# Linear attention, cosine FFN and soft MoE in one kernel: when the w_out tiles of the first blocks are converted, and how they meet phi

## The chip, the core and the metric

The kernel runs on one core of a Trainium2 chip. Five engines work from queues of their own: TensorE (PE, with its weight loads shown as PEld), VectorE (DVE), ScalarE (ACT), GpSimd (POOL) and SyncE (SP, which here only issues DMAs). The metric is the device time of one execution in microseconds, the median of three runs for the kernel before.

## What is computed

```python
# q, k, v: (8, 8, 576, 64); everything is fp32
kv = einsum('bhsd,bhse->bhde', k, v)
out = einsum('bhsd,bhde->bhse', q, kv)
x = out / sqrt(mean(out * out, -1) + 1e-6) * g_norm        # -> (4608, 512)
h = x @ w_in                                               # (4608, 2048)
x2 = (h * cos(h)) @ w_out                                  # (4608, 512)
logits = x2 @ phi                                          # (4608, 32)
d = softmax(logits, axis=0)                                # over the tokens
c = softmax(logits, axis=1)                                # over the slots
slots = (d.T @ x2).reshape(8, 4, 512)
slot_out[e] = relu(slots[e] @ w1[e]) @ w2[e]
return c @ slot_out.reshape(32, 512)
```

`w_in` and `w_out` come in as float64 values whose bits the kernel turns into fp32 itself.

## The kernel before

The 4608 tokens are twelve blocks j of 384 tokens. A block's x is held transposed as a high and a low part (`xt`), and the 2048 columns of `w_in` are sixteen tiles f of 128. One main step (j, f) is `main`: 12 products of 128 x 128 weights with 384 tokens (high x high, high x low, low x high, four chunks each) into one PSUM bank `h`. Then ScalarE scales and rounds (`fr_tt`), VectorE takes the remainder (`round_off`, L403), ScalarE the sine (`cos_b`), VectorE multiplies by h (`cos_c`, L417) into `gT`.

`w_out` is never multiplied out for each token: the logits are gT times the small matrix wp = w_out @ phi, one 128 x 32 piece per tile f. `wp_kk` (L320) and `wp_sum` (L329) make that piece: four products with 32 columns of phi as weights, each into its own group of 32 PSUM partitions, a copy to SBUF (`wq`), and a product with `rep32`, which adds the four groups; a copy stores the piece in `wp`. `logits2` (L468) multiplies two tiles' gT with their pieces, block 0 into partitions 0 to 63 and block 1 into 64 to 127 of one bank (`l`).

Blocks 0 and 1 are interleaved: step f of the start does main step (0, f) and, from f = 4 on (`L=4`), (1, f-4). In the same steps the sixteen tiles of `w_in` (letters A R P L H S: scale on ScalarE, three bit operations on VectorE, high part on ScalarE, low part on GpSimd) and of `w_out` (a r p l: scale on ScalarE, the three bit operations on VectorE) are converted. The order inside a step is written out by hand in the strings `one` (steps 0 to 3) and `two`, and before step 0 in `start`; each letter is one call. `LI` and `LO` say how many tiles ahead of the step w_in and w_out are converted. Side work is hung on steps by `at2`: `wp_kk(f)` on step f + `wT` = f, `wp_sum(f)` on f + `wM` = f + 1, `logits2(j, f)` on f + 3 + 4j, the transposition of gT (`gtr`) one or two steps after its main step. The raw w_out tiles wait in three buffers (`ro`), so a load on SP's queue waits until the tile three before it is converted, and what is behind it on that queue waits too.

In the start the first batch's kv products, `att_out` (`ops`), `att_xs`, `att_xT` (`xTps`) and `att_lo` prepare block 0's x. The second batch's kv products run in step 0; `ke` says which engine copies them from PSUM (0 ScalarE, 1 VectorE).

Of the kernel before, what the change touches and what calls it, by code (L numbers as in the profile page):

```python
# [19 lines left out]
SIGN_BIT = -0x80000000  # L20

PLAN = dict(
    ke=(0, 1),
    lp=(0, 0, 0),
    wE=0,
    gE=(0, 0),
    nt=(1, (12, 16, 20, 24), (1, 2), (2, 1), (3, 1), 4),
    rx=0,
    nq=(0, 0),
    nl=3,  # L30
    wT=0,
    wM=1,
    E=((20, 21, 5, 1), (17, 19, 4, 2)),
    F=((23, 25), (22, 24)),
    L=4,
    LI=2,
    LO=2,
    PI=2,
    PO=2,
    PS=1,  # L40
    stop=None,
    start=(
# [17 lines left out]
    A=(((1, 2, 2), (1, 1, 1), (3, 3, 4), (0, 1, 0)), ((9, 10, 12), (0, 0, 0), (11, 13, 14), (0, 0, 0)), ((8, 11, 11), (1, 1, 1), (11, 14, 14), (1, 0, 0))),  # L60
# [14 lines left out]
def tile_linear_attention__ffn_cos__soft_moe(  # L75
# [15 lines left out]
    nc = tc.nc  # L91
    B, H, D = kv.shape[0], 8, 64
    NF, KD = w_in.shape[0], w_in.shape[2]
    NS = phi.shape[2]
    NB = qT.shape[0]
    TB = qT.shape[3]

    SP = 2
    const = ctx.enter_context(tc.tile_pool(name="const", bufs=1))
# [36 lines left out]
    def at_bank(name):  # L136
        return ps_a.tile([128, 512], F32, tag="at", name=name)

    def copy_on(e, out, in_):
        (nc.vector.tensor_copy if e else nc.scalar.copy)(out=out, in_=in_)  # L140
# [9 lines left out]
        return [(0, 64, 2 * p), (64, 64, 2 * p + 1)]  # L150

    def load_q(j):
        t = q_p.tile([128, 4, TB], F32, tag=f"q{j % 2}", name="q")
        if j == 0:
            for t3 in range(3):
                nc.sync.dma_start(out=t[:, :, t3 * 128:(t3 + 1) * 128], in_=qT[j][:, :, t3 * 128:(t3 + 1) * 128])
        else:
            nc.sync.dma_start(out=t, in_=qT[j])
        q_t[j] = t
# [38 lines left out]
    def att_out(j, t):  # L198
        ps = at_bank("ops")
        for pr in range(4):  # L200
            for p0, n, b in spans(j):
                assert (b, pr) in kv_done
                c0 = t * 128 + p0
                nc.tensor.matmul(out=ps[p0:p0 + n, pr * 128:(pr + 1) * 128],  # L204
                                 lhsT=q_t[j][:, pr, c0:c0 + n], rhs=kvbd[b % 2][:, pr, :],
                                 start=True, stop=True)
# [55 lines left out]
    first = {}  # L262

    def stage():
        ta = t_p.tile([128, 6, 512], F32, tag="TA", name="st_a")
        tb = t_p.tile([128, 6, 512], F32, tag="TB", name="st_b")
        sp = const.tile([128, SP, 512], F32, tag="sp", name="st_m")
        first["sx"] = x_p.tile([128, 6, 512], F32, tag="x1", name="st_x")
        first["sp"] = sp
        first["ex"] = const.tile([128, 512], F32, tag="ex", name="st_n")  # L270
        first["wi"] = [sp[:, i, :] for i in range(2)]
        first["wo"] = [ta[:, i, :] for i in range(3)]
        tf = ta.rearrange("p a c -> p (a c)")
        first["wq"] = [tf[:, 1536 + 128 * i:1664 + 128 * i] for i in range(2)]
        ring.extend([None, tf[:, 1792 + TB * i:1792 + TB * (i + 1)], 1] for i in range(3))
        first["ro"] = [tb[:, 2 * i:2 * i + 2, :].rearrange("p a c -> p (a c)").bitcast(I32).rearrange(
            "p (c t) -> p c t", t=2) for i in range(3)]

    def load_wout(f):
        t = first["ro"][f % 3]  # L280
        nc.sync.dma_start(out=t, in_=w_outT[f].bitcast(I32).rearrange("p k (c t) -> p (k c) t", t=2))
        raw_t[NF + f] = t
        loaded.add(NF + f)
# [31 lines left out]
        hi, lo = (w_t[f][:, i].rearrange("p k c -> p (k c)") for i in range(2))  # L315
        nc.gpsimd.tensor_tensor(out=lo, in0=T, in1=hi.bitcast(F32), op=ALU.subtract)  # L316

    wq_t, wp_done = {}, set()

    def wp_kk(f):  # L320
        assert ("L", f, 1) in done
        ps = at_bank("wps")
        for kk in range(KD):
            nc.tensor.matmul(out=ps[32 * kk:32 * kk + 32, 0:128], lhsT=phi_sb[:, kk, :],
                             rhs=first["wo"][f % 3][:, kk * 128:(kk + 1) * 128], start=True, stop=True)
        copy_on(PLAN["wE"], first["wq"][f % 2], ps[:, 0:128])
        wq_t[f] = ps

    def wp_sum(f):  # L329
        ps = wq_t.pop(f)[:, 128:128 + NS]  # L330
        nc.tensor.matmul(out=ps, lhsT=first["wq"][f % 2], rhs=rep32, start=True, stop=True)
        nc.scalar.copy(out=wp[:, f, :], in_=ps)
        wp_done.add(f)

# [456 lines left out]
    def at2(j, f, *a):  # L791
        at(*U(j, f), *a)
# [14 lines left out]
    def ld_at(j, f, fn, *a):  # L807
        loads.setdefault(U(j, f), []).append((fn, a))

    for j in range(NB):  # L810
        for f in range(NF):
            if on_pe(j, f):
                at2(j, f + (1 if j == 1 and f < NF // 2 else 2), gtr, j, f)
        for h in range(2):
            if (j, h) == (NB - 2, 1):
                for x in range(4):
                    ld_at(NB - 1, x + PLAN["lag"], regroup, j, h, (x,))
            elif not on_pe(j, 8 * h):
                for x in range(4):
                    ld_at(j, PLAN["rg"][h] + x * PLAN["rx"], regroup, j, h, (x,))  # L820
        if j == 0:
            for f in range(NF):
                at2(0, f + PLAN["wT"], wp_kk, f)
                at2(0, f + PLAN["wM"], wp_sum, f)
        if j < 2:
            for f in range(0, NF, 2):
                late_in = j and f + 3 + L >= NF - (L < 6)
                at2(*((1, f + 3) if late_in else (0, f + 3 + L * j)), logits2, j, f)
        if j < NB - 1:
            for c in range(4 * (j > 1)):  # L830
# [150 lines left out]
    with tc.manual_schedule():  # L981
        stage()
        make_identity(nc, ident)
        nc.vector.memset(mhalf, -0.5)
        for i in range(2):
            nc.vector.memset(kz[64 - 64 * i:128 - 64 * i, i], 0.0)
        for t in kvab:
            nc.gpsimd.memset(t, 0.0)
        for t in PLAN["start"].split():
            token(t, 0)  # L990
            if t == "q.0":
                nc.sync.dma_start(out=gn, in_=gn2)
                nc.sync.dma_start(out=phi_sb, in_=phi)
        nc.vector.tensor_reduce(out=rep32, in_=ident.rearrange("p (j s) -> p s j", s=NS), axis=AX.X, op=ALU.add)
        nc.vector.tensor_copy(out=rep, in_=rep32.rearrange("p (o s) -> p o s", o=1).to_broadcast([128, 4, NS]))
        for f in range(NF):
            if f + PLAN["LI"] + 2 < NF and f + PLAN["LI"] + 2 not in loaded:
                ld_at(0, f, load_win, f + PLAN["LI"] + 2)
            if f + PLAN["LO"] + 1 < NF and f + PLAN["LO"] + 1 + NF not in loaded:
                ld_at(0, f, load_wout, f + PLAN["LO"] + 1)  # L1000
        for f in range(NF):
            for t in (PLAN["one"] if f < L else PLAN["two"]).split():
                token(t, f)
# [25 lines left out]
def _lay_out(q, k, v, g_norm, moe_w_in, moe_w_out, moe2_phi, moe2_w1, moe2_w2):  # L1029
# [6 lines left out]
    for p in range(B // 2):  # L1036
# [8 lines left out]
    w_out = moe_w_out.reshape(16, P, 512)  # L1045
    w_outT = moe_w_out.reshape(16, P, 4, P).transpose(0, 3, 2, 1)
    return {
        "qT": np.stack(blocks),
        "kv": kvm,
        "kvr": kvr,  # L1050
        "gn2": np.concatenate([g_norm, g_norm]).reshape(P, 1),
# [31 lines left out]
```

## Time and profile before

| | us |
|---|---|
| median of three runs | 705.47 (705.43 to 707.11) |
| the profiled execution, its own time | 705.78 |
| its span, first to last instruction | 703.9 |

The rows below come from that one execution. In the rows of a time line the columns are the start, how long it took, engine, line, operation, output<-input, shape, count and, in brackets, the engine's idle time before and what ended it. TensorE's products in fp32 take two passes each, those of `h` (fp32r) and transpositions one. A table by stage shows for each stretch its length, then busy time and instructions of each engine, the granted TensorE clock as a share of the upper of its two levels (2.4 GHz; the lower is 1.2), the DMA share and GB/s. In the chain of waits each piece is start, length, engine, tile and line.

### The profile page before, as it was taken

To read this page: it belongs to the slowest core of one execution; us is meant where nothing else is said; L and a number is where in the kernel's file an instruction comes from. 1 tells how busy PE (TensorE), PEld (TensorE's weight loads), DVE (VectorE), ACT (ScalarE), POOL (GpSimd) and SP (SyncE) were. 2 spreads that over 40 slices of the span, in tenths; PEclk is the share of its full clock that TensorE was granted. 3 is DMA by queue.
4 is the path that set the end of the run, shared out by engine and by line. 5 is a ranking of instruction groups with operands and counts; after the bars stand their busy time and mean duration, and the time that the engine had idled before them with its cause. 6 is when DMAs were issued, how large, how long until landed. Compare 5 with 4: busy or idle time off the path is not lost.

```text
span 703.9 us, 13646 instructions
## 1 busy us (share of the span) xinstructions
PE 675.8 (96%) x5103; PEld 558.7 (79%) x5103; DVE 525.1 (75%) x1100; ACT 441.6 (63%) x931; POOL 106.2 (15%) x104
## 2 busy tenths in 40 slices
PE   7769999999999999999999999999999999999994
PEld 6659998886988887988888879888978787874364
DVE  3998998467888878888888888888887875444144
ACT  3577998675667675675576765756757567661143
POOL 2342333100402111112012021110120210000500
PEclk9999999999999999999999999999999999999996
DMA  9963442022742674574435845735349278989998
GB/s 316 393 209 132 180 171 100 1 85 96 209 130 76 186 187 140 168 198 107 136 81 159 208 141 160 213 93 150 85 108 327 70 233 268 346 302 346 393 360 358
DMA packets 69297, 134.12 MB, mean 191 GB/s; under 512 B 8433, under 2 KB 41841, under 8 KB 68465
## 3 DMA queue, kind: packets, MB, share of 16 engines
q1 hardware_dynamic: 69232, 133.27, 59.7%
q8 instruction: 40, 0.66, 0.4%
q14 instruction: 25, 0.20, 0.1%
HBM read 91.29 MB, written 13.63 MB: 149 GB/s over the span
## 4 chain that ended last, share of the span: by engine, by line
PE 71%; DVE 12%; ACT 10%; DMA 4%; issue 2%; SPq 0%; DVEq 0%; ACTq 0%
PE h L378 43%; PE ab L553 5%; PE l L465 4%; PE ops L204 3%; DVE gT L417 3%; ACT fr L408 3%; DVE tt L403 2%; PE xTps L236 2%; DVE tr L423 2%; PE tr L438 2%; PE eo L706 2%; PE eh L680 2%; ACT L408 1%; ACT L513 1%; DMA st_b<-in_w_outT 1%
## 5 line engine op out<-in xcount | busy, mean ns | idle before, releaser
L378 PE MATMUL h<-xt,w 128*128 128x384 f32 x2304 | 438.7, 342 | 1.0 <-DVE xt L249 0.4
L378 PEld LDWEIGHTS h<-xt,w 128*128 128x128 f32 x2304 | 397.0, 188 | 31.6 <-issue 12.2
L408 ACT ACTIVATE fr<-tt 128x384 f32<-128x384 f32 x192 | 100.4, 524 | 135.8 <-DVE tt L403 135.4
L417 DVE TENSOR_TENSOR gT<-fr,h 128x384 f32<-128x384 f32 x186 | 102.7, 553 | 58.3 <-ACT fr L408 58.1
L216 POOL TENSOR_TENSOR ri<-ss,mhalf 128x8 f32<-128x8 f32 x36 | 65.6, 1826 | 421.4 <-DVE ss L214 421.4
L403 DVE SCALAR_TENSOR_TENSOR tt<-tt,fr 128x384 f32<-128x384 f32 x192 | 106.1, 557 | 25.9 <-ACT tt L398 24.4
L398 ACT ACTIVATE tt<-fr 128x384 f32<-128x384 f32 x192 | 100.8, 525 | 6.1
L396 ACT ACTIVATE fr<-h 128x384 f32<-128x384 f32 x192 | 92.3, 481 | 14.2 <-PE h L378 14.1
L423 DVE STREAM_TRANSPOSE tr<-gT 128x384 f32<-128x384 f32 x144 | 83.3, 579 | 5.1 <-DVE gT L417 0.2
L240 ACT ACTIVATE xt<-xTps,gn 128x512 fp32r<-128x512 f32 x36 | 24.5, 683 | 25.8 <-PE xTps L236 25.8
L204 PE MATMUL ops<-kvA,q 128*64 128x128 f32 (+1 forms) x384 | 38.2, 278 | 1.4 <-ACT g L140 1.3
L204 PEld LDWEIGHTS ops<-kvA,q 128*64 128x64 f32 (+1 forms) x384 | 33.8, 164 | 5.4 <-issue 2.8
L249 DVE SCALAR_TENSOR_TENSOR xt<-xTps,gn,xt 128x512 fp32r<-128x512 f32 x36 | 26.4, 738 | 12.0 <-ACT xt L240 11.8
L316 POOL TENSOR_TENSOR w<-st_m,w 128x512 fp32r<-128x512 f32 x16 | 26.4, 1648 | 53.8 <-ACT w L311 42.1
L553 PE MATMUL ab<-g,d 128*32 128x512 f32 x288 | 33.5, 596 | 0.4 <-DVE d L535 0.4
L465 PE MATMUL l<-gT,wp 128*32 128x384 f32 x312 | 33.3, 498 | 0.0
L140 ACT COPY g<-tr 128x384 f32<-128x384 f32 (+1 forms) x64 | 23.4, 392 | 6.7 <-PE tr L438 6.3
L184 PEld LDWEIGHTS kvps<-kv 128*64 128x64 f32 x512 | 17.6, 138 | 11.8 <-issue 7.0
L213 DVE TENSOR_REDUCE ss<-sq 128x8 f32<-128x512 f32 x33 | 22.1, 671 | 5.0 <-ACT sq L211 4.8
L184 PE MATMUL kvps<-kv 128*64 128x64 f32 x512 | 20.7, 226 | 3.7 <-DMA kv<-in_kv 2.0
L225 DVE TENSOR_TENSOR xs<-ops,ri 128x512 f32<-128x512 f32 x33 | 22.3, 681 | 2.4 <-POOL ri L216 2.4
L211 ACT ACTIVATE sq<-ops 128x512 f32<-128x512 f32 x33 | 19.5, 590 | 7.2 <-PE ops L204 7.2
(139 smaller groups left out, 626.3 us busy)
## 6 DMA issues: line engine op xcount, KB each, us to landing
g<-tr SPq DMA_DIRECT2D x288, 96.0 KB
kv<-in_kv SPq DMA_DIRECT2D x32, 512.0 KB
ew<-in_w SPq DMA_DIRECT2D x19, 512.0 KB
out<-ot SPq DMA_DIRECT2D x12, 768.0 KB
q<-in_qT SPq DMA_DIRECT2D x11, 768.0 KB
rw<-in_w_in SPq DMA_DIRECT2D x16, 512.0 KB
st_b<-in_w_outT SPq DMA_DIRECT2D x16, 512.0 KB
ew<-in_w SPq DMA_DIRECT2D x6, 1024.0 KB
```

Of the source, the lines that this page charges most:

```text
L184: nc.tensor.matmul(out=ps[h], lhsT=t[:, 0, r, h], rhs=t[:, 1, r, h], start=(r == 0), stop=False)
L204: nc.tensor.matmul(out=ps[p0:p0 + n, pr * 128:(pr + 1) * 128], lhsT=q_t[j][:, pr, c0:c0 + n], rhs=kvbd[b % 2][:, pr, :], start=True, stop= ...
L216: nc.gpsimd.tensor_tensor(out=ri[:, :, 0], in0=ss, in1=mhalf, op=ALU.pow)
L378: nc.tensor.matmul(out=ps, lhsT=w[:, a, kk, :], rhs=x[:, b, kk, :], start=(n == 0), stop=(n == 3 * KD - 1))
L396: nc.scalar.activation(out=fr, in_=ps, func=AF.Copy, bias=0.25, scale=INV_2PI)
L398: nc.scalar.activation(out=tt, in_=fr, func=AF.Copy, bias=ROUND_M)
L403: nc.vector.scalar_tensor_tensor(out=tt, in0=tt, scalar=-ROUND_M, in1=fr, op0=ALU.add, op1=ALU.subtract)
L408: nc.scalar.activation(out=fr, in_=tt, func=AF.Sin, scale=-TWO_PI_DOWN)
L417: nc.vector.tensor_tensor(out=g, in0=fr, in1=h_t.pop((j, f)), op=ALU.mult)
L423: nc.vector.transpose(out=tr_t[j, h][:, :, o, :], in_=g.rearrange("p (b t) -> p b t", t=32))
L465: nc.tensor.matmul(out=l_t[j][32 * o:32 * o + 32, :], lhsT=wp[:, f, :], rhs=gT_t.pop((j, f)), start=(c == 0), stop=(c == (2 if j == NB - 1 ...
L553: nc.tensor.matmul(out=ps[32 * c:32 * c + 32, :], lhsT=d[:, t, :], rhs=gs[c // 2][t][:, (c % 2) * 512:(c % 2) * 512 + 512], start=(t == 0) ...
```

## The change

w_out tile f is converted in step f instead of f - 2 (`LO=0`, `PO=0`), so the calls a.0 to l.1 leave `start`, and the last two tiles are converted in steps 14 and 15. Its product with phi stands in step f + 2 (`wT=2`) and is made in another way: the four chunks of the tile are the weights (128 x 128 each), phi's 32 columns move, and the four products add up in PSUM; `wp_sum`, the copy `wq` and its product with `rep32` are gone. The logits of block 0 stand one step later (f + 4); those of block 1 stay (f + 7). The copies of the second batch's kv go to ScalarE. q is laid out by 128 tokens, so that the first block's three loads have segments of 2 KB instead of 512 B. A sine on a small constant stands first in ScalarE's queue, `rep32` and `rep` are made at the start, the last raw tile has a buffer of its own, gT has one more buffer (the space of `wq`), and one transposition (block 1, f = 8) stands a step later.

```diff
 PLAN:
-    ke=(0, 1),
+    ke=(0, 0),
-    wE=0,
-    wT=0,
-    wM=1,
+    wT=2,
-    LO=2,
+    LO=0,
-    PO=2,
+    PO=0,
 start:
-        "lo.0 xs.2 A.1 H.0 S.0 warm.4 a.0 lo.1 xT.2 warm.8 R.1 P.1 r.0 win.3 a.1 L.1 lo.2 H.1 r.1 p.0 S.1 p.1 "
-        "l.0 l.1 "
+        "lo.0 xs.2 A.1 H.0 S.0 warm.4 lo.1 xT.2 warm.8 R.1 P.1 win.3 L.1 lo.2 H.1 S.1 "
...
-        t = q_p.tile([128, 4, TB], F32, tag=f"q{j % 2}", name="q")
+        t = q_p.tile([128, 3, 4, 128], F32, tag=f"q{j % 2}", name="q")
-                nc.sync.dma_start(out=t[:, :, t3 * 128:(t3 + 1) * 128], in_=qT[j][:, :, t3 * 128:(t3 + 1) * 128])
+                nc.sync.dma_start(out=t[:, t3], in_=qT[j][:, t3])
...
     def wp_kk(f):
         assert ("L", f, 1) in done
-        ps = at_bank("wps")
+        ps = at_bank("wps")[:, 0:NS]
         for kk in range(KD):
-            nc.tensor.matmul(out=ps[32 * kk:32 * kk + 32, 0:128], lhsT=phi_sb[:, kk, :],
-                             rhs=first["wo"][f % 3][:, kk * 128:(kk + 1) * 128], start=True, stop=True)
-        copy_on(PLAN["wE"], first["wq"][f % 2], ps[:, 0:128])
-        wq_t[f] = ps
-
-    def wp_sum(f):
-        ps = wq_t.pop(f)[:, 128:128 + NS]
-        nc.tensor.matmul(out=ps, lhsT=first["wq"][f % 2], rhs=rep32, start=True, stop=True)
+            nc.tensor.matmul(out=ps, lhsT=first["wo"][f % 3][:, kk * 128:(kk + 1) * 128], rhs=phi_sb[:, kk, :],
+                             start=(kk == 0), stop=(kk == KD - 1))
         nc.scalar.copy(out=wp[:, f, :], in_=ps)
...
-                at2(j, f + (1 if j == 1 and f < NF // 2 else 2), gtr, j, f)
+                at2(j, f + (1 if j == 1 and f < NF // 2 else 3 if (j, f) == (1, NF // 2) else 2), gtr, j, f)
...
-                at2(*((1, f + 3) if late_in else (0, f + 3 + L * j)), logits2, j, f)
+                at2(*((1, f + 3) if late_in else (0, f + 4 + (L - 1) * j)), logits2, j, f)
...
+        table = sm_p.tile([128, 2], F32, tag="sb", name="table")
+        nc.scalar.activation(out=table[:, 0:1], in_=mhalf[:, 0:1], func=AF.Sin)
```

TensorE's queue of the kernel before, from the main products of step 5 of the interleaved blocks to those of step 7 (`tr` transposes gT, `wps` is the product with phi, `l` the logits, `h` the main products):

```order
L378 MATMUL h<-xt,w 128x384 x24
L438 MATMUL tr<-ident,gT 128x128 x6
L331 MATMUL wps<-rep_106,st_a 128x32
L324 MATMUL wps<-st_a,phi_sb 32x128 x4
L378 MATMUL h<-xt,w 128x384 x24
L438 MATMUL tr<-ident,st_a 128x128 x3
L438 MATMUL tr<-ident,gT 128x128 x3
L331 MATMUL wps<-rep_106,st_a 128x32
L324 MATMUL wps<-st_a,phi_sb 32x128 x4
L474 MATMUL l<-gT,wp 32x384 x3
L474 MATMUL l<-st_a,wp 32x384
L378 MATMUL h<-xt,w 128x384 x24
```

The same place in the changed kernel:

```order
L369 MATMUL h<-xt,w 128x384 x24
L429 MATMUL tr<-ident,gT 128x128 x6
L321 MATMUL wps<-phi_sb,st_a 128x32 x4
L465 MATMUL l<-gT,wp 32x384 x2
L369 MATMUL h<-xt,w 128x384 x24
L429 MATMUL tr<-ident,st_a 128x128 x3
L429 MATMUL tr<-ident,gT 128x128 x3
L321 MATMUL wps<-phi_sb,st_a 128x32 x4
L465 MATMUL l<-gT,wp 32x384
L465 MATMUL l<-st_a,wp 32x384
L369 MATMUL h<-xt,w 128x384 x24
```

The products with phi of one tile stand as four 128-wide ones in a row, and the two blocks' logits, which stood as four products in every other step, stand as two in every step.

VectorE's queue of the kernel before, from the second w_in tile's bit operations to gT of step 0 (`st_m` is a w_in tile, `st_a` a w_out tile, `xt` the low part of x, `kvA` the second batch's kv, `tt` and `gT` step 0's):

```order
L305 SCALAR_TENSOR_TENSOR st_m<-rw,st_m 128x512
L249 SCALAR_TENSOR_TENSOR xt<-xTps,gn,xt 128x4x128
L295 TENSOR_SCALAR st_a<-st_a 128x512
L300 SCALAR_TENSOR_TENSOR st_a<-st_b,st_a 128x512 x2
L305 SCALAR_TENSOR_TENSOR st_a<-st_b,st_a 128x512 x2
L994 TENSOR_REDUCE rep_106<-ident 128x32
L995 COPY rep<-rep_106 128x128
L295 TENSOR_SCALAR st_m<-st_m 128x512
L300 SCALAR_TENSOR_TENSOR st_m<-rw,st_m 128x512
L403 SCALAR_TENSOR_TENSOR tt<-tt,fr 128x384
L305 SCALAR_TENSOR_TENSOR st_m<-rw,st_m 128x512
L295 TENSOR_SCALAR st_a<-st_a 128x512
```

The same place in the changed kernel:

```order
L302 SCALAR_TENSOR_TENSOR st_m<-rw,st_m 128x512
L245 SCALAR_TENSOR_TENSOR xt<-xTps,gn,xt 128x4x128
L292 TENSOR_SCALAR st_m<-st_m 128x512
L297 SCALAR_TENSOR_TENSOR st_m<-rw,st_m 128x512
L394 SCALAR_TENSOR_TENSOR tt<-tt,fr 128x384
L302 SCALAR_TENSOR_TENSOR st_m<-rw,st_m 128x512
L292 TENSOR_SCALAR st_a<-st_a 128x512
L297 SCALAR_TENSOR_TENSOR st_a<-st_b,st_a 128x512
L408 TENSOR_TENSOR gT<-fr,h 128x384
```

The bit operations of two w_out tiles and the two `rep` instructions no longer stand ahead of the third w_in tile, and no copies of kvA stand ahead of gT.

## Rows read from the trace of the kernel before

**Rows 1.** The page: busy time of TensorE, share of the span, instructions.

```profile
PE 675.8 (96%) x5103; PEld 558.7 (79%) x5103; DVE 525.1 (75%) x1100; ACT 441.6 (63%) x931; POOL 106.2 (15%) x104
```

**Rows 2.** The table by stage: PE, PEld, DVE, ACT, POOL, clock, DMA.

```profile
24.00:47.50 23.50, 17.40 (x200) 15.63 (x199) 23.05 (x48) 16.66 (x36) 8.90 (x6) 1.00 0.76 283
47.50:53.30 5.80, 2.70 (x25) 1.61 (x21) 5.77 (x10) 2.80 (x7) 2.34 (x3) 1.00 0.84 256
53.30:60.20 6.90, 6.88 (x39) 6.79 (x38) 5.32 (x9) 3.56 (x8) 1.18 (x1) 0.75 0.45 164
...
71.90:113.00 41.10, 41.10 (x316) 37.32 (x317) 40.62 (x71) 38.71 (x105) 12.81 (x7) 1.00 0.46 165
113.00:130.00 17.00, 17.00 (x132) 14.70 (x129) 11.60 (x23) 11.38 (x27) 5.11 (x3) 1.00 0.19 64
...
147.00:640.00 493.00, 490.05 (x3542) 411.09 (x3544) 381.53 (x847) 317.81 (x645) 52.98 (x36) 1.00 0.58 169
```

**Rows 3.** The chain that ended last, in order of time: start, length, what.

```profile
54.37 5.40 PE h L378 x24
...
60.60 0.63 PE l L474 x4
...
66.74 4.39 PE h L378 x24
...
71.78 0.14 PE wps L331 x2
71.93 0.36 PE wps L324 x8
72.28 0.65 PE l L474 x8
...
126.48 0.77 PE l L474 x4
```

**Rows 4.** The time line of TensorE's products: one step, and the tail.

```profile
59.93 0.31 PE L331 MATMUL wps<-rep,st_a 128*128 128x32 f32 x2
...
642.24 0.98 PE L668 MATMUL sT<-rep,part 128*128 128x32 f32 x8
643.05 0.69 PE L643 MATMUL warm<-ident 128*128 128x128 f32 x4
```

**Rows 5.** The source line L331: passes, with shortest, median and longest in ns.

```profile
L331 PE MATMUL wps<-rep,st_a x32: 192/235/277, 34.6 to 130.1; 128*128 128x32 f32 x32
```

**Rows 6.** The time line of GpSimd and VectorE, 20 to 36 us.

```profile
20.90 1.33 POOL L316 TENSOR_TENSOR w<-st_m,w 128x512 fp32r<-128x512 f32 x1 [1.75 <-ACT w L311]
21.13 1.65 DVE L300 SCALAR_TENSOR_TENSOR st_m<-rw,st_m 128x512 int32<-128x512 int32 x1
...
28.69 0.42 DVE L295 TENSOR_SCALAR st_m<-st_m 128x512 int32<-128x512 int32 x1
29.15 0.69 DVE L300 SCALAR_TENSOR_TENSOR st_m<-rw,st_m 128x512 int32<-128x512 int32 x1
29.76 0.55 DVE L403 SCALAR_TENSOR_TENSOR tt<-tt,fr 128x384 f32<-128x384 f32 x1
...
31.16 1.92 DVE L140 COPY kvA<-kvps 64x64 f32<-64x64 f32 x8
...
33.83 0.55 DVE L417 TENSOR_TENSOR gT<-fr,h 128x384 f32<-128x384 f32 x1
...
35.97 0.55 DVE L403 SCALAR_TENSOR_TENSOR tt<-tt,fr 128x384 f32<-128x384 f32 x1
```

**Rows 7.** The time line of ScalarE, 23 to 27 us.

```profile
23.05 0.69 ACT L290 ACTIVATE st_a<-st_b 128x512 f32<-128x512 f32 x1 [0.98 <-DMA st_b<-in_w_outT]
...
24.34 0.66 ACT L290 ACTIVATE st_m<-rw 128x512 f32<-128x512 f32 x1
...
26.65 0.49 ACT L396 ACTIVATE fr<-h 128x384 f32<-128x384 f32 x1 [1.64 <-PE h L378]
```

More of the change, by code (lines that the diff above doesn't have):

```diff
@@ L95, in tile_linear_attention__ffn_cos__soft_moe @@
     NB = qT.shape[0]
-    TB = qT.shape[3]
+    TB = qT.shape[2] * qT.shape[4]
     SP = 2
@@ L202, in att_out @@
                 assert (b, pr) in kv_done
-                c0 = t * 128 + p0
                 nc.tensor.matmul(out=ps[p0:p0 + n, pr * 128:(pr + 1) * 128],
-                                 lhsT=q_t[j][:, pr, c0:c0 + n], rhs=kvbd[b % 2][:, pr, :],
+                                 lhsT=q_t[j][:, t, pr, p0:p0 + n], rhs=kvbd[b % 2][:, pr, :],
                                  start=True, stop=True)
@@ L273, in stage @@
         tf = ta.rearrange("p a c -> p (a c)")
-        first["wq"] = [tf[:, 1536 + 128 * i:1664 + 128 * i] for i in range(2)]
-        ring.extend([None, tf[:, 1792 + TB * i:1792 + TB * (i + 1)], 1] for i in range(3))
+        ring.extend([None, tf[:, 1536 + TB * i:1536 + TB * (i + 1)], 1] for i in range(4))
         first["ro"] = [tb[:, 2 * i:2 * i + 2, :].rearrange("p a c -> p (a c)").bitcast(I32).rearrange(
@@ L280, in load_wout @@
         t = first["ro"][f % 3]
+        if f == NF - 1:
+            t = q_p.tile([128, KD * 128, 2], I32, tag="q1", name="st_q")
         nc.sync.dma_start(out=t, in_=w_outT[f].bitcast(I32).rearrange("p k (c t) -> p (k c) t", t=2))
@@ L316, in cv_lo @@
         nc.gpsimd.tensor_tensor(out=lo, in0=T, in1=hi.bitcast(F32), op=ALU.subtract)
-    wq_t, wp_done = {}, set()
+    wp_done = set()
     def wp_kk(f):
         assert ("L", f, 1) in done
-        ps = at_bank("wps")
+        ps = at_bank("wps")[:, 0:NS]
         for kk in range(KD):
-            nc.tensor.matmul(out=ps[32 * kk:32 * kk + 32, 0:128], lhsT=phi_sb[:, kk, :],
-                             rhs=first["wo"][f % 3][:, kk * 128:(kk + 1) * 128], start=True, stop=True)
-        copy_on(PLAN["wE"], first["wq"][f % 2], ps[:, 0:128])
-        wq_t[f] = ps
-    def wp_sum(f):
-        ps = wq_t.pop(f)[:, 128:128 + NS]
-        nc.tensor.matmul(out=ps, lhsT=first["wq"][f % 2], rhs=rep32, start=True, stop=True)
+            nc.tensor.matmul(out=ps, lhsT=first["wo"][f % 3][:, kk * 128:(kk + 1) * 128], rhs=phi_sb[:, kk, :],
+                             start=(kk == 0), stop=(kk == KD - 1))
         nc.scalar.copy(out=wp[:, f, :], in_=ps)
@@ L823, in tile_linear_attention__ffn_cos__soft_moe @@
                 at2(0, f + PLAN["wT"], wp_kk, f)
-                at2(0, f + PLAN["wM"], wp_sum, f)
         if j < 2:
@@ L984, in tile_linear_attention__ffn_cos__soft_moe @@
         nc.vector.memset(mhalf, -0.5)
+        table = sm_p.tile([128, 2], F32, tag="sb", name="table")
+        nc.scalar.activation(out=table[:, 0:1], in_=mhalf[:, 0:1], func=AF.Sin)
+        nc.vector.tensor_reduce(out=rep32, in_=ident.rearrange("p (j s) -> p s j", s=NS), axis=AX.X, op=ALU.add)
+        nc.vector.tensor_copy(out=rep, in_=rep32.rearrange("p (o s) -> p o s", o=1).to_broadcast([128, 4, NS]))
         for i in range(2):
@@ L993, in tile_linear_attention__ffn_cos__soft_moe @@
                 nc.sync.dma_start(out=phi_sb, in_=phi)
-        nc.vector.tensor_reduce(out=rep32, in_=ident.rearrange("p (j s) -> p s j", s=NS), axis=AX.X, op=ALU.add)
-        nc.vector.tensor_copy(out=rep, in_=rep32.rearrange("p (o s) -> p o s", o=1).to_broadcast([128, 4, NS]))
         for f in range(NF):
@@ L998, in tile_linear_attention__ffn_cos__soft_moe @@
                 ld_at(0, f, load_win, f + PLAN["LI"] + 2)
-            if f + PLAN["LO"] + 1 < NF and f + PLAN["LO"] + 1 + NF not in loaded:
-                ld_at(0, f, load_wout, f + PLAN["LO"] + 1)
+            if f + PLAN["LO"] + 2 < NF and f + PLAN["LO"] + 2 + NF not in loaded:
+                ld_at(0, f, load_wout, f + PLAN["LO"] + 2)
         for f in range(NF):
@@ L1047, in _lay_out @@
     return {
-        "qT": np.stack(blocks),
+        "qT": np.stack(blocks).reshape(12, P, 4, 3, P).transpose(0, 1, 3, 2, 4),
         "kv": kvm,
```

## The prediction

> **What bounds the kernel now.** I read the page first: TensorE is busy 96% of the span [rows 1]. Then the stage table, since the diff touches only the start and the two interleaved blocks. In it the stretch from 24 to 53.3 us belongs to VectorE, busy 23.05 of 23.50 and 5.77 of 5.80 us, while TensorE has 2.70 of 5.80 in its second part. From there the roles change: TensorE is busy 41.10 of 41.10 us between 71.9 and 113, and 17.00 of 17.00 up to 130 [rows 2]. VectorE is nearly full there too (40.62), but TensorE shows no wait, and the pieces of the chain of waits are TensorE's alone, step after step: transpositions, `wps`, sometimes `l`, then 24 passes of `h` in 4.39 us [rows 3]. After the interleaved blocks TensorE stays busy 490.05 of 493.00 us [rows 2], so a shift at 147 us is handed to the end undiminished. Hence two rules for the sum: until about 54 us, count what delays VectorE; from 54 us to the last main step of the second block, count TensorE time.
>
> **The start (gain).** Six VectorE instructions of the tiles 0 and 1 of `w_out` and the eight copies of the second batch (1.92 us) leave VectorE's queue, with `rep` put ahead of all data, where VectorE is still idle. The gain isn't their sum, because VectorE then waits for others. Step by step, from [rows 6, 7]: the L300 that ends at 22.78 is followed at once by L305 and the x rest, so the first `h` and with it ScalarE's `fr` move from 26.65 to about 26.3. The third `w_in` tile's scaling on ScalarE (24.34, 0.66) has no `w_out` scaling in front and starts near 23.95, so its L295 starts near 24.6 rather than at 28.69. `tt` of step 0 then has only ScalarE's two instructions of about 0.5 us to wait for: 27.35 instead of 29.76. Before the sine ScalarE now has one scaling (0.66) and the eight copies (taken at the 1.92 us that VectorE needs), but no table load (moved to the very start, where ScalarE has nothing else): it starts near 29.8, and `gT` of step 0 stands near 30.3 instead of 33.83, 3.5 us earlier. Between it and `tt` of step 1 stand four conversion instructions of 0.4 to 0.7 us, one of which will meet GpSimd's subtraction. What such a meeting costs is seen at 21.13: an L300 of 0.69 us (so long where it meets nothing) took 1.65, ending just after GpSimd's 1.33 us [rows 6]. That puts `tt` of step 1 between 32.4 and 33.3, against 35.97. From there to 53.3 VectorE's order is the same and it is full [rows 2], so the lead is kept. I take **-3.0 us**, between the two; bounds -1.5 (if data of the second batch or of `w_in` come only just in time) and -4.0.
>
> Longer q segments (2 KB for 512 B) shorten three issues and three transfers ahead of the first attention rows; VectorE's start is set by GpSimd's powers and its own queue, so 0 (0 to -0.5). The 16 ScalarE copies that vanish are worth 0: ScalarE is busy 38.71 of 41.10 and TensorE doesn't wait for it [rows 2]. The conversions of tiles 14 and 15 now run in a stretch where VectorE is busy 11.60 of 17.00 us [rows 2], which covers their six instructions of 0.4 to 0.7 us; without that cover they'd cost 3.6. On SP's queue a `w_out` load now waits for a conversion two steps later, and the `w_in` loads behind it with it; those are issued steps ahead of use, so 0 (up to +1). The transposition moved by one step is the same work, 0.
>
> **The product with phi (loss).** Before, a tile cost a first half (four products of 32 columns side by side, 0.36) and a second half (0.14), 0.50 together on the chain [rows 3]. The changed form, four accumulating products with the 128 x 128 tile as weights and 32 columns of phi moving, isn't in the stretch, but the tail has exactly it: `sT`, 8 passes, from 642.24 to the next instruction at 643.05, **0.81 us**, about 0.10 a pass [rows 4]. Each pass moves only 32 columns but has 128 weight columns to load. A lower bound is the second pass of L331, which with its weights loaded ahead added 0.03 to the first (0.31 for both [rows 4], up to 0.277 for one [rows 5]): 8 x 0.03 = 0.25. I take 0.81, the same shape in a queue just as full. By the order of the built program 13 products stand after step 4 (tiles 3 to 15), where before 11 first and 12 second halves stood: 13 x 0.81 - 11 x 0.36 - 12 x 0.14 = 10.53 - 5.64 = **+4.9 us**.
>
> The Trainium skill, TensorEngine Tiling (Array Packing), When to Use Tiling, speaks against this edit: for a moving side of 32 columns it advises swapping the operands and tiling four columns wide, which is what the kernel does now and what the change undoes. By that rule the change loses, and the two prices above, 0.50 and 0.81, agree. By its page TensorE: Matmul & The Clock Gate, LDWEIGHTS, a load takes columns / 1.2 ns, 107 ns for 128; by that estimate a tile costs 0.85 and the term is +5.4 instead of +4.9.
>
> **The logits of the first block (loss).** Their groups are moved one step later. Before, in steps 7, 9, 11 and 13 a group of block 0 and one of block 1 stood together and used the four column groups side by side: 8 passes in 0.65, while 4 passes alone took 0.63 [rows 3]. So the second was free. Now the blocks' groups fall into alternate steps and each is paid. Behind instructions that use all 128 columns a group costs 0.77 [rows 3], behind L324 0.64. In the stretch: before 9 places (6 x 0.64 + 3 x 0.77 = 6.15), after 13 places, each behind full-width work (13 x 0.77 = 10.01): **+3.9 us** (+2.5 if the extra 0.12 doesn't appear).
>
> **Sum.** -3.0 + 4.9 + 3.9 = +5.8 us. The profiled execution itself took 705.78 us (span 703.9), 0.3 above the median of 705.47; on the median the changed kernel comes to about **711.2 us**, 0.8% slower.
>
> **Rivals.**
> *The weight loads run ahead.* If TensorE loads the next tile's weights while earlier passes move, a pass costs 0.03 and the product term is 13 x 0.25 - 5.64 = -2.4; with -3.0 and +3.9 the kernel is 1.5 us faster, 704.0: not slower. It decides where a pass costs under 0.046 us (13 x 8 x 0.046 = 4.7 makes the sum zero). For it: L331's second pass. Against: all eight of `sT`, and that nothing long stands between the eight passes. The Trainium skill, TensorE: Matmul & The Clock Gate, Architectural detail, says that TensorE's queue pulls weight loads ahead of matmuls in flight; by that rule this rival holds, and 0.81 for `sT` says it doesn't reach further than one load.
> *The start gains more and the clock doesn't fall.* Between 53.3 and 60.2 the granted clock was 0.75 on average, after TensorE had been busy for 2.70 of 5.80 us [rows 2]; 24 passes of `h` took 5.40 instead of 4.39 [rows 3]. The changed order puts a longer product and the first logits into that idle time. If the clock stays at its upper level (2.4 GHz) throughout, that gives back 1.0 to 1.4, and with a start gain of 4.0 the sum is +3.4: 708.9.
> *The start gains nothing*, because the loads of the second batch or of `w_in` bind once VectorE is ahead: -0.5 + 8.8 = +8.3, 713.8. Against: the load that ScalarE waited for there (0.98 at 23.05 [rows 7]) is one of `w_out`, which the change needs later.
>
> **How the numbers follow.** Forecast 0.72, less weight load 0.07, better start 0.12, no gain at the start 0.06, and 0.03 for a start gain beyond 4 together with short passes (faster). 0.3% of 705.47 is 2.1 us, about what a measurement can tell: the forecast and the better and worse starts are slower, the first rival counts as no change. A little of the forecast's and the better start's spread falls below 2.1 us. Slower 0.86, same 0.09, faster 0.05. The range takes the forecast with its bounds (start -1.5 to -4.0, logits +2.5 to +3.9, a product 0.75 to 0.85) and the better start, and leaves out the first rival and the worst start: 707.6 to 713.2.
>
> **What would show it.** Right: the first main step of the interleaved pair (54.0 now) starts near 51; eight `wps` passes show about 0.8 us per tile on the chain; `l` stands in every step from 6 to 14 with four passes; a step takes about 6.6 us rather than 5.54 and 6.18 in turn; VectorE's share in the stretch falls to some 87% while TensorE's stays at 100%. Wrong: passes of `wps` at 0.03 to 0.05, groups of `l` that still overlap, or a TensorE that waits in the stretch.

## The result and the profile after

The changed kernel takes 713.44 us (median, 712.85 to 715.27) where the kernel before takes 705.54 beside it: ratio 1.0107, 95% interval 1.0090 to 1.0123. It is slower, by 7.9 us at the medians. The forecast was 711.2, in a range of 707.6 to 713.2. The profiled execution took 713.43 us, its span is 711.6; that of before took 705.78 and 703.9.

The page's part 1 of the changed kernel (against [rows 1]):

```profile
PE 686.6 (96%) x5071; PEld 567.6 (80%) x5071; DVE 526.3 (74%) x1092; ACT 440.7 (62%) x923; POOL 105.8 (15%) x104
```

TensorE is busy 10.8 us longer with 32 instructions fewer, so its work has become dearer. The table by stage (columns as in [rows 2]) shows where:

```profile
44.60:48.00 3.40, 1.04 (x4) 0.64 (x4) 3.37 (x5) 0.69 (x1) 2.63 (x2) 0.50 0.53 163
48.00:54.80 6.80, 6.41 (x26) 5.14 (x27) 5.69 (x9) 2.80 (x7) 1.27 (x1) 0.50 0.28 93
...
74.70:121.00 46.30, 46.30 (x304) 41.03 (x303) 41.54 (x71) 38.16 (x96) 12.04 (x8) 1.00 0.46 160
121.00:138.00 17.00, 17.00 (x124) 14.88 (x124) 11.12 (x22) 9.92 (x23) 3.99 (x3) 1.00 0.00 1
155.00:648.00 493.00, 489.98 (x3545) 410.76 (x3547) 381.58 (x846) 317.81 (x644) 52.99 (x36) 1.00 0.59 169
```

Two things stand here. From 44.6 to 54.8 us the granted clock is 0.50, its lower level of 1.2 GHz. From 74.7 to 138 TensorE never waits, and from 155 on the two kernels are alike (489.98 of 493 us busy, before 490.05). The chain of waits of the changed kernel, first the stretch before step 4, then one whole step:

```profile
47.57 0.69 DVE xs L221
...
48.39 1.09 PE xTps L232 x4
49.48 0.64 PE tr L429 x3
50.12 1.55 PE wps L321 x8
51.67 1.43 PE l L465 x4
53.09 1.05 PE xTps L232 x4
54.14 4.55 PE h L369 x24
...
66.34 4.39 PE h L369 x24
70.73 0.65 PE tr L429 x6
71.38 0.81 PE wps L321 x8
72.20 0.77 PE l L465 x4
72.97 4.39 PE h L369 x24
```

A step is 6.63 us now (66.34 to 72.97). The new product is 0.81 per tile, and a group of four logits passes, 0.77, stands in every step. In the half-clock stretch the same product takes 1.55 and the same group 1.43. The `...` marks stand for pieces left out.

To see where time is won and lost in any of the kernels below, I read four starts of `h` from the time line of TensorE: of step 3 (the last one in the start), of steps 4 and 5 (the first two of the interleaved pair) and of the first main step of block 2, behind the pair. Each row is one execution, and not all on the same chip.

| us | step 3 | step 4 | step 5 | block 2 | step 5 to block 2 |
|---|---|---|---|---|---|
| before | 42.38 | 54.02 | 61.16 | 143.89 | 82.73 |
| after | 38.88 | 53.79 | 59.67 | 151.63 | 91.96 |
| new product alone | 41.26 | 54.63 | 62.16 | 147.92 | 85.76 |
| after, logits meet | 38.96 | 51.23 | 59.17 | 147.53 | 88.35 |
| start's edits alone | 41.91 | 54.08 | 60.79 | 143.52 | 82.73 |
| after, old product, logits meet | 38.65 | 50.95 | 57.60 | 143.07 | 85.47 |
| after, fitted added products | 38.19 | 49.91 | 55.77 | 147.72 | 91.94 |
| after, tiny added products | 39.30 | 50.55 | 56.63 | 148.57 | 91.94 |

The changed kernel leads by 3.5 us at step 3, by 0.2 at step 4 and 1.5 at step 5, and then loses 9.2 us in the pair. The question for the runs: are these 9.2 us the product and the logits, and where did the lead go?

### The profile page after: what moved, and what is told of

It is laid out like the page before. It is cut to its first block, busy times and chain, and to the rows that moved or that the text cites. A ratio compares the mean times of both kernels' runs of the same rounds, so it can differ in the third digit from the quotient of the medians.

```text
span 711.6 us, 13581 instructions
## 1 busy us (share of the span) xinstructions
PE 686.6 (96%) x5071; PEld 567.6 (80%) x5071; DVE 526.3 (74%) x1092; ACT 440.7 (62%) x923; POOL 105.8 (15%) x104
## 4 chain that ended last, share of the span: by engine, by line
PE 73%; DVE 11%; ACT 10%; DMA 2%; issue 2%; SPq 1%; POOL 0%; DVEq 0%; ACTq 0%
PE h L369 42%; PE ab L544 5%; PE l L456 4%; PE ops L200 3%; PE xTps L232 3%; DVE gT L408 2%; ACT fr L399 2%; PE tr L429 2%; DVE tt L394 2%; PE eo L697 2%; PE eh L671 2%; PE l L465 2%; DVE tr L414 2%; PE wps L321 2%; PE fo L722 2%
## 5 line engine op out<-in xcount | busy, mean ns | idle before, releaser
L456 PE MATMUL l<-gT,wp 128*32 128x384 f32 x312 | 33.3, 498 | 0.0
L232 PE MATMUL xTps<-ident,xs 128*128 128x128 f32 x132 | 21.7, 291 | 4.3 <-DVE xs L221 2.7
L232 PEld LDWEIGHTS xTps<-ident,xs 128*128 128x128 f32 x132 | 16.1, 147 | 11.3 <-issue 4.4
```

The costliest lines, as they stand in the source:

```text
L232: nc.tensor.transpose(ps[:, kk * 128:(kk + 1) * 128], xs[:, kk * 128:(kk + 1) * 128], ident)
L456: nc.tensor.matmul(out=l_t[j][32 * o:32 * o + 32, :], lhsT=wp[:, f, :], rhs=gT_t.pop((j, f)), start=(c == 0), stop=(c == (2 if j == NB - 1 ...
```

## Experiments

Each kernel ran in five rounds beside the kernel before on its chip. There, in 80 executions of it on three chips, the times reached from 703.3 to 709.9 us, so ratios are compared, and small terms are read from the starts of `h` above.

### The product alone

```diff
 (kernel before)
-    wp_kk: four 32-column groups, copy to wq;  wp_sum: product with rep32
+    wp_kk: 4 products, lhsT=first["wo"][f % 3][:, kk*128:(kk+1)*128], rhs=phi_sb[:, kk, :], into ps[:, 0:NS]
```

> The kernel before, with the new product alone: eight passes per w_out tile with the tile stationary, straight into 32 columns of PSUM, no copy of a quarter sum and no second product; conversions, copies and the order of the logits as before. Theory of the prediction (every pass pays for its weight load, 0.81 us a tile): 11 x 0.81 - 11 x 0.36 - 12 x 0.14 = +3.3 us over the kernel before, near 708.8 us, and eight passes of 0.81 in the chain at the end of each step. Rival (the loads run ahead of the passes, about 0.25 us a tile): 11 x 0.25 - 5.6 = -2.9 us, near 702.6 us.

Measured: 710.05 us, ratio 1.0059 (1.0037 to 1.0080), so +4.2 us with an interval of 2.6 to 5.6. From step 5 to block 2 it lost 85.76 - 82.73 = 3.0 us, from step 4 on 3.4. One step of its chain:

```profile
72.97 0.81 PE wps L324 x8
73.78 0.78 PE l L468 x8
```

0.81 per tile, 0.1 per pass: no pass gets near the 0.03 of the rival on loads that run ahead, and its 702.6 is out.

### The logits put side by side again

```diff
 (changed kernel)
-    at2(..., (0, f + 4 + (L - 1) * j)), logits2, j, f)
+    at2(..., (0, f + (7 if j else 5))), logits2, j, f)
```

> The changed kernel, with the logits of block 0 one step later (with the fifth step after their tile instead of the fourth), so that in four steps the groups of block 0 and block 1 stand next to each other again. Theory (the logits' term of the prediction is the lost meeting): two groups apart cost 2 x 0.77 us, a meeting 0.65 us, so 4 x 0.89 = 3.6 us come back: near 709.9 us. Rival (a group costs what it costs behind a tile-stationary product, whatever stands beside it, or VectorE, 90% busy there, takes over the bound): no change, 713.4 us.

Measured: 709.86 us, ratio 1.0049 (1.0031 to 1.0067), 4.1 us under the changed kernel's ratio. From step 5 to block 2 it is 91.96 - 88.35 = 3.6 us shorter, the expected size: four meetings at 0.9. Its chain:

```profile
70.79 0.78 PE l L465 x8
71.57 4.39 PE h L369 x24
...
77.43 4.25 PE h L369 x24
```

Eight passes of two blocks take 0.78, and the next step has none. By the pieces a meeting saves 2 x 0.77 - 0.78 = 0.76. The step without a group also has the shorter `h`, 4.25 for 4.39, which makes up the 0.9.

### The start's edits alone

```diff
 (kernel before)
-    ke=(0, 1),
+    ke=(0, 0),
 table of the sine and rep32/rep made at the start; q as [128, 3, 4, 128], loaded by t3
```

> The kernel before, with the start's changes alone: the copies of block 1 on ScalarE's side of the split, the sums of the identity and the sine table ahead of the first work, q by 128 tokens; product, conversions of w_out and logits as before. Theory (these edits give VectorE its lead): gT of the first tile 2 to 3 us before 33.8 us; with the clock falling as it does before, h of step 4 1.5 us earlier, near 704.0 us; without a fall near 702.5 us. Rival (the lead comes from the conversions that moved out of the start, not from these edits): no change, 705.5 us.

Measured: 705.16 us, ratio 0.9971 (0.9952 to 0.9991). In the trace `h` of step 3 leads by 0.5 us and that of step 5 by 0.4, while that of step 4, for which 1.5 was expected, doesn't lead. VectorE's time line around gT of the first tile:

```profile
25.25 0.41 DVE L294 TENSOR_SCALAR st_a<-st_a 128x512 int32<-128x512 int32 x1
25.58 2.38 DVE L299 SCALAR_TENSOR_TENSOR st_a<-st_b,st_a 128x512 int32<-128x512 int32 x2
27.89 1.28 DVE L304 SCALAR_TENSOR_TENSOR st_a<-st_b,st_a 128x512 int32<-128x512 int32 x2
...
32.58 0.55 DVE L416 TENSOR_TENSOR gT<-fr,h 128x384 f32<-128x384 f32 x1 [0.22 <-ACT fr L407]
```

The `w_out` conversions (`st_a`) still stand ahead, 4.1 us of VectorE, and gT comes at 32.58: 1.25 us ahead of [rows 6], not the 2 to 3 expected; the changed kernel has 30.42. So most of the lead comes from the conversions that left the start, as the rival said. But the rival's "no change" missed too: by the ratio these edits won 0.6 to 3.4 us, more than the 0.4 of the one trace, and what the rest is stays open. Which of the bundled edits gives it was not taken apart either.

### The old product in the changed order

```diff
 (changed kernel)
+    wp_kk and wp_sum as in the kernel before, wT=2, wM=3, one buffer wq of its own
+    logits at f + 5 and f + 7, as in the run above
```

> The changed kernel with the old product (four products side by side, copy of the four groups, sum one step later) and with block 0's logits in the fifth step after their tile, so that they meet block 1's again; conversions of w_out two steps later, the start and the copies as changed. Theory (product and logits are the whole loss): the product gives back 13 x (0.81 - 0.50) = 4.0 us, the logits 3.6 us as measured, together 7.6 us: near the kernel before, ratio 1.000, and gT of the first tile stands 3.5 us earlier than there, which shows that the late conversions give the lead, since the other edits of the start alone gave 0.95 us at the second h. Rival (the changed order of conversions itself costs time in the interleaved steps): ratio over 1.004.

Measured: 706.60 us, ratio 1.0007 (0.9989 to 1.0025). The theory holds: without the new product and the lost meetings the loss is gone. `h` of step 5 stands 3.6 us ahead of the kernel before. But the pair takes 2.7 us longer than there (85.47 for 82.73). A part of it must be the products and logits that left the start and now stand where TensorE is the bound; how much was not taken apart. And there is a wait that neither the kernel before nor the changed one has:

```profile
130.43 1.97 POOL ri L214
...
132.41 0.70 DVE xs L223
...
133.25 0.52 PE tr L439 x3
```

With shorter steps TensorE reaches the transpositions before the attention row's power (`ri`) and scaling (`xs`) are through; the waits name 0.8 us for `tr` on `xs`.

### Added products that keep TensorE busy before step 4

Four kernels put products that nobody reads into the places where TensorE waits, to see whether the clock stays up and whether the lead then arrives.

```diff
 (changed kernel; att_xT, block 1)
+    12 products of ident x ident ahead of t=0, 16 ahead of t=1
```

> The changed kernel, with 28 small products of the identity added that nobody reads: 12 ahead of the first and 16 ahead of the second group of block 1's transposes, where TensorE has nothing to do (42.9 to 48.4 us). Theory (the gain of the start was eaten by the granted clock at half from 44.61 to 54.85 us): the clock stays up, transposes, product and logits from 48.39 take about 3.1 instead of 5.76 us, the first h of step 4 starts near 51.5 to 52 instead of 53.8, and the time falls by 2.0 to 2.9 us to 710.5 to 711.4 us. Rival (VectorE's chain sets the start of step 4, the clock only shows that TensorE idles): h still starts near 53.8, 713.4 us.

Measured: 715.02 us, ratio 1.0129 (1.0099 to 1.0160). The added products were too long:

```profile
48.30 3.57 PE xTps L233 x32
51.87 0.44 PE xTps L235 x4
...
54.80 4.17 PE h L372 x24
```

The clock stayed up, and from the second transposes to `h` the same pieces took 2.93 us (51.87 to 54.80) against 5.75 (48.39 to 54.14). So the price of the half clock was as expected, but the products had pushed those transposes back by 3.5 us, and the time missed its range. The next run was cut to fit.

```diff
 (changed kernel)
+    7 products of ident x ident ahead of the product of tile 1, 12 ahead of t=1
```

> The changed kernel, with the added products that nobody reads cut to fit the two places where TensorE waits: 7 ahead of the second tile's product (42.4 to 43.9 us), 12 between the first and the second group of block 1's transposes (45 to 47.6 us). The run before showed the granted clock staying up and the stretch from those transposes to the first h of step 4 taking 2.9 instead of 5.75 us, but its longer row of added products pushed the transposes back by 3.5 us. Theory (the half clock is what ate the start's lead): the second transposes stand near 48.4 as in the changed kernel, h of step 4 near 51.5, and the time falls by 2 to 3 us, to about 0.997 of the changed kernel, 1.007 of the kernel before. Rival (VectorE's low parts of block 1's x, which stand at 53.0 and 54.9, are what the second h of step 4 waits for): the first h comes earlier, but it waits there, and less than 1 us is won.

Measured: 712.28 us, ratio 1.0098 (1.0073 to 1.0124); its profiled execution, 711.29, is the shortest of six that reach to 713.99. The expected 1.007 was missed. Its stage from 48 us:

```profile
48.00:54.80 6.80, 6.62 (x42) 5.61 (x42) 6.73 (x10) 4.61 (x10) 1.28 (x1) 1.00 0.41 131
```

The clock stayed up, `h` of step 5 leads the kernel before by 5.4 us instead of 1.5, and the pair takes the same 91.94 us. Of the 3.9 us won by then only 2.2 are in the span (709.4 for 711.6): behind the last main product this execution is 1.7 us longer. All kernels with 14 to 28 added products have that, and one more instruction fetch. The next run made the added work of 8 wide instructions, the one after it of 19 tiny ones.

```diff
 (changed kernel, the same two places)
+    e12_wide: 3 and 5 products of ident x 512 columns
+    e14_pad:  7 and 12 products of 32 x 32 of ident
```

> The changed kernel with the two added stretches of products that nobody reads made of 8 wide instructions (512 columns of a finished w_in tile) instead of 19 narrow ones. In the runs with added products h of step 5 came up to 5.4 us earlier than in the kernel before, but each of the four shows one more instruction fetch (41 for 40), which falls 64 to 71 us behind the last main product, into the output's stores, and the stretch from the last main product to the end is 80.2 to 80.8 us instead of 79.2. Theory (the added instructions pushed the program over one more fetch): with 8 there are 40 fetches, a tail of 79.2 us, no half clock before step 4, and the time falls by 2 to 4 us against the changed kernel: ratio 1.005 to 1.008. Rival (the longer tail belongs to the clock or to the chip): tail of 80 us or more, ratio 1.010.

> The changed kernel with 19 products of 32 columns that nobody reads, in the same two places: as many instructions as in the run with fitted products, but hardly any work. Theory of the fetch: 41 fetches, a tail of 80.2 to 80.8 us from the last main product to the end, the granted clock at half as in the changed kernel, time 1.0 to 1.6 us over the changed kernel, ratio 1.012. Rival: tail of 79.2 us and the changed kernel's time, ratio 1.0107.

Measured: 712.51 us, ratio 1.0091 (1.0069 to 1.0112) with the wide ones; 715.13 us, ratio 1.0120 (1.0094 to 1.0146) with the tiny ones. The instruction queue in the page's part 3, wide first, then tiny (each from its own page):

```profile
q8 instruction: 40, 0.66, 0.4%
```

```profile
q8 instruction: 41, 0.67, 0.4%
```

From the last start of `h` to the end of the span (the changed kernel: 711.6 - 632.4 = 79.2): 79.2 us with 40 fetches, 80.8 with 41. The fetch theory holds; the last fetch falls 71 us behind the last `h`, while the output's stores fill the DMA engines, and the tail is 1.6 us longer. The table by stage shows how it ends, from 3.4 to 1.5 us before the end of the span, first the changed kernel, then the tiny products (the last two columns are the DMA share and GB/s):

```profile
708.24:710.14 1.90, 0.00 (x0) 0.00 (x0) 0.00 (x0) 0.00 (x0) 0.00 (x0) 0.50 1.01 414
```

```profile
706.68:708.58 1.90, 0.00 (x0) 0.00 (x0) 0.00 (x0) 0.00 (x0) 0.00 (x0) 0.50 0.24 97
```

With 40 fetches the stores run at full rate to the end; with 41 a few packets are left over when the rest is done: 78 to 220 GB/s in this stretch in the five kernels with 41. That these are packets held up by the extra fetch is likely, but not shown.

The wide run kept the clock up, as expected, and missed its time for another reason: a wide product took 0.87 us (4.36 for 5 on the chain), where the logits' passes (0.77 for four of 384 columns) would make it 0.51, and the products pushed the transposes back to 50.44.

The tiny products hold the surprise. They are hardly any work, a half clock was expected, and yet the profiled execution, again the shortest of its six (711.85 to 716.01), has none in these stretches:

```profile
44.60:48.00 3.40, 1.88 (x31) 1.61 (x32) 3.37 (x7) 1.11 (x3) 3.40 (x3) 1.00 0.44 141
48.00:54.80 6.80, 6.42 (x43) 5.43 (x42) 6.73 (x12) 4.90 (x10) 1.68 (x2) 1.00 0.45 150
```

```profile
47.65 0.66 PE xTps L235 x4
48.30 0.33 PE tr L436 x3
48.63 0.81 PE wps L328 x8
49.44 0.77 PE l L472 x4
50.21 0.60 PE xTps L235 x4
...
52.66 0.75 DVE xt L248
...
53.45 2.20 PE h L376 x11
```

The five TensorE pieces take 3.16 us at the upper level and 5.75 at the lower, and `h` of step 5 leads by 4.5 us. So the size of the clock's price is shown: 2.93, 2.93 and 3.16 us in three executions at the upper level (the long, the wide and the tiny products). That the added work keeps the clock up is not shown. Nor can the price in the medians be told: with the wide and the fitted products the ratios are within the interval of the changed kernel's, and of the changed kernel's own four executions the longest, 715.27, has the highest mean clock, 0.988 for 0.980 to 0.982.

Not all of that lead is the clock. GpSimd's powers `ri` took 3.80 us here for 3.24 in the kernel before and the changed one, so its subtraction began only after `tt` of step 3, which took 0.55 us instead of 1.62:

```profile
46.44 0.55 DVE L401 SCALAR_TENSOR_TENSOR tt<-tt,fr 128x384 f32<-128x384 f32 x1
```

The same holds for the fitted products and for the old product in the changed order, and gives each 1.1 us on VectorE. Why `ri` took longer stays open.

The chain also shows what comes next once the clock is up: VectorE's low part of block 1's x (`xt` at 52.66) sets the second `h` of step 4.

### The same on the other kernels

```diff
 e10_quarter_fit: old product in the changed order, with the 7 and 12 products of ident
 e11_start_fit:   start's edits alone, with 6 products ahead of tile 3's product and 8 ahead of t=1
```

> The same as the last, with the added products that nobody reads at the two places where TensorE waits (7 ahead of the second tile's product, 12 between the first and second transposes of block 1). Theory: with the clock kept up the start's lead reaches step 4: 2 to 3 us faster than the last, ratio 0.996 to the kernel before. Rival (VectorE's low parts set step 4): the same as the last.

> The kernel before with the start's edits alone, as run above (ratio 0.997), and with added products that nobody reads at the two places where TensorE waits there: 6 ahead of the fourth tile's product, 8 between the first and second transposes of block 1. Theory: the fall of the clock at 52.4 us goes, h of the first step of the pair takes 4.2 to 4.4 instead of 4.97 us and the transposes 0.6 instead of 1.05: 1.0 to 1.3 us faster than without, ratio 0.9955. Rival (the fall stays, or the added products push the transposes): the same as without, 0.997.

Measured: 709.10 and 706.76 us, ratio 1.0041 (1.0025 to 1.0057) and 1.0013 (0.9996 to 1.0030), both slower than without the added products (1.0007 and 0.9971). Both have 41 fetches and tails of 80.2 and 80.4 us. Both times missed. In the first the products pushed the transposes (its `h` of step 5 stands at 59.24, without them at 57.60), and the tail came on top. In the second the clock stayed up and `h` of step 5 came 1.1 us earlier than without (59.70 for 60.79), as its theory said, but the tail took back 1.3. That makes 0.2 us more; the ratios differ by 3.0, and the rest stays open.

### The late groups side by side too

```diff
+    steps from 15 on: block 0's and block 1's logits behind the transpositions, next to each other
```

> The changed kernel with the old product and the logits in the fifth step (run above, ratio 1.0007), and with the last groups of block 0's logits put beside block 1's, so that seven groups meet instead of four. Theory: 3 x 0.89 = 2.7 us less, ratio 0.997, the lead of 3.6 us at step 5 kept down to about 3.5 us at the end. Rival (something else ends the last interleaved steps): 1.0007.

> The kernel before with the start's edits alone (run above, ratio 0.997), and with the last groups of the two blocks' logits side by side, so that six meet instead of four. Theory: 2 x 0.89 = 1.8 us less than without, ratio 0.9946. Rival (the late groups are covered): 0.997.

Measured: the changed order with the old product 705.16 us, ratio 0.9990 (0.9974 to 1.0006); the start's edits alone 703.88 us, ratio 0.9962 (0.9947 to 0.9977). From step 5 to block 2 the first takes 83.93 us and wins 85.47 - 83.93 = 1.54 us of the expected 2.7; of the rest, 0.6 is TensorE's wait for `xs`, which grows from 0.8 to 1.4 us. Its lead at step 5 was only 0.9 us in this execution (60.27), with the half clock again from 45.7 to 55.9 us. The second wins 82.73 - 81.19 = 1.54 of 1.8. Its chain, where two groups of 0.77 stood in the kernel before:

```profile
133.27 0.66 PE tr L437 x6
133.93 0.78 PE l L473 x8
```

The second is the version to keep: the kernel before, the start's edits, and six meetings of the logits, 2.7 us faster than the kernel before and 10 faster than the changed one, by the ratios. That the two meetings make it faster than the start's edits alone (0.9971) shows in the trace, not in the ratios, whose intervals overlap.

## Why the prediction was right, and where not

**Direction and loss: right.** The two losing terms were +4.9 and +3.9, together 8.8, counted from step 4 on. From `h` of step 4 to block 2 the changed kernel takes 7.97 us longer (97.84 for 89.87). In this stretch it gains 0.85 by the clock, because `h` of step 4 took 5.40 us in the kernel before [rows 3] and 4.55 here; without that the loss is 8.8, as forecast. (From step 5 on it is 9.2: the product and the group of step 4, which the kernel before pays at 0.50 + 0.63 and the changed one at 0.81, lie ahead of it.) The pieces are those named: 0.81 per tile, as `sT` in [rows 4] had it, and a group of 0.77 in every step from 6 to 14, as the one piece behind full-width work in [rows 3]. Each was taken back by itself: the product alone cost 3.0 to 3.4 us where 3.3 was worked out for its eleven tiles, the meetings gave 3.6.

**What was costed at nothing: right.** TensorE shows no wait from 74.7 to 138 us. The conversions of the last two tiles found VectorE busy 11.12 of 17.00 us, ScalarE is busy 38.16 of 46.30. A step of 6.6 us was forecast and is 6.63; VectorE's share is 90%, not 87%.

**The start: mis-sized, and the failed step is the rule "until about 54 us, count what delays VectorE".** The first main step of the pair was to start near 51, 3.0 us earlier. It starts at 53.79, only 0.2 us earlier; with the 0.85 that it then gains in `h` the start is worth 1.1, under the lower bound of 1.5. Two things went into that.

First, VectorE's own lead was 2.3 us and not 3.0. gT of step 0 stands at 30.42 (30.3 forecast), but `tt` of step 1 at 33.65, 2.3 us ahead of 35.97 [rows 6], where 32.4 to 33.3 was worked out. The meeting with GpSimd that was priced came and cost 1.1 us:

```profile
31.52 1.48 DVE L292 TENSOR_SCALAR st_m<-st_m 128x512 int32<-128x512 int32 x1
...
33.65 0.55 DVE L394 SCALAR_TENSOR_TENSOR tt<-tt,fr 128x384 f32<-128x384 f32 x1
```

From there "the lead is kept" held on VectorE: it is still 2.3 us at `xs` and at gT of step 3 (50.96; before 53.27). VectorE meets GpSimd again, at `tt` of step 2 (1.63 us) and of step 3 (1.62), but the kernel before has the same meetings at the same places (1.62 both), so they take nothing from the lead. Step 3 in the changed kernel, VectorE, then GpSimd:

```profile
46.03 1.62 DVE L394 SCALAR_TENSOR_TENSOR tt<-tt,fr 128x384 f32<-128x384 f32 x1
47.57 1.28 DVE L221 TENSOR_TENSOR xs<-ops,ri 128x512 f32<-128x512 f32 x2
```

```profile
45.89 1.33 POOL L313 TENSOR_TENSOR w<-st_m,w 128x512 fp32r<-128x512 f32 x1
```

The kernel before:

```profile
48.33 1.62 DVE L403 SCALAR_TENSOR_TENSOR tt<-tt,fr 128x384 f32<-128x384 f32 x1
49.87 1.27 DVE L225 TENSOR_TENSOR xs<-ops,ri 128x512 f32<-128x512 f32 x2
```

```profile
48.20 1.33 POOL L316 TENSOR_TENSOR w<-st_m,w 128x512 fp32r<-128x512 f32 x1
```

Second, TensorE didn't pick this lead up. The second transpositions of block 1 still start 2.2 us earlier (48.39; before 50.60). But from there to `h` of step 4 the chain of the changed kernel is TensorE's own work at half clock: two transpositions of x, one of gT, a product and a group of logits, 5.75 us for 3.16 or less at the upper level. In the kernel before the same way takes 3.8 us (50.60 to 54.37), 1.0 of it a wait for VectorE; its first group of logits stands ahead of it. The forecast took TensorE's work in that gap as idle time of a VectorE-bound stretch, and the clock as before, where its fall cost 1.0 in `h` [rows 3]. In the profiled execution of the changed kernel it fell earlier and stayed down longer. The rival on the clock only looked at a gain.

**The sum.** In the trace it is -0.2 - 0.85 + 8.8 = +7.7 us, and 713.43 - 705.78 = 7.65 in the profiled times, against +5.8. The median is 0.2 above the range's upper end of 713.2; by the ratio, on the 705.47 that the forecast started from, it is 713.0. That it lies at this end and not beyond is in part luck: the start missed its bound by 0.4, and the range had 0.5 to spare for a product dearer than 0.81, which didn't come.

**The rivals.** Passes at 0.03, by weight loads that run ahead, are excluded by the product alone. The Trainium skill, TensorE: Matmul & The Clock Gate, LDWEIGHTS, gave an estimate of 0.85 per tile; the chain's 0.81 agrees with it. By the Trainium skill, TensorE: Matmul & The Clock Gate, Architectural detail, TensorE's queue can pull loads ahead of matmuls in flight; at 0.10 a pass the new product shows no gain from that. The rule to swap the operands of a narrow product (the Trainium skill, TensorEngine Tiling (Array Packing), When to Use Tiling) holds in the runs: between the kernel whose logits meet (ratio 1.0049) and the one that has the old product as well (1.0007) lie 3.0 us by the ratios and 2.9 by their traces from step 5 to block 2. The better start shows only in single executions of the kernels with added products (4.5 and 5.4 us at step 5), with 1.1 us of it from `tt`, and not in their medians. In number the rival of a start that gains nothing, 713.8, came nearest, but not by its mechanism: no load binds VectorE, whose three waits between 24 and 31 us (0.65, 0.94 and 0.57) all end on ScalarE.

## What to carry to other kernels

Work that leaves a stretch where another engine is the bound and lands in one where TensorE is full has to be counted at its full price, and groups of narrow products that share the array are worth keeping next to each other: each lost meeting cost 0.9 us, and two more made the pair 1.5 us shorter in the trace of the kernel before with the start's edits. A lead on VectorE is not a lead until TensorE has picked it up: list what TensorE still has to do in the gap, and price it at both of its clock levels. Before judging an edit by one or two microseconds, look at the number of instruction fetches and where the last one falls.

## What the runs showed of the hardware

- With one more instruction fetch, 41 for 40, the last of them in the output's stores, the stretch behind the last main product was 80.2 to 80.9 us for 79.2. That was so in all five kernels with 41, on three chips, one of them with hardly any added work, and in none of the nine with 40.
- The granted clock before step 4 can't be read off TensorE's busy time from 41.3 to 44.6 us alone. The changed kernel was busy 1.78 of these 3.30 us and fell to 0.50 at 44.6; the changed order with the old product and added products was busy 1.41 of them and stayed at 1.00 (3.08 of the next 3.40 us busy, against 1.04). What decides it stays open here. The table by stage, the changed kernel first:

```profile
41.30:44.60 3.30, 1.78 (x16) 1.63 (x14) 3.23 (x9) 3.11 (x7) 1.91 (x2) 1.00 0.20 81
```

```profile
41.30:44.60 3.30, 1.41 (x11) 1.27 (x9) 3.23 (x8) 2.74 (x6) 1.53 (x1) 1.00 0.36 140
```

- A group of four logits passes takes 0.77 us behind full-width work and 0.63 behind narrow products; eight passes of both blocks take 0.78 and 0.65. The second block's passes are free either way.
- A VectorE instruction that met GpSimd's subtraction took 1.48 and 1.62 us for 0.42 and 0.55, also the one with a single tensor input (L292). The meeting at `tt` is in the kernel before as well.
